# Packing two dQ blocks into one PSUM bank, with a new order of the backward attention loop

## The chip, the cores and the metric

The kernel runs on one core of one Trainium2 chip. The metric is the device time of one execution in microseconds (us); three runs of the kernel before gave 2509.24, 2516.67 and 2526.46 us, so the median is 2516.67 us. Durations and waits are read from one profiled execution, whose span is 2517.6 us.

## The reference

The reference is a transformer block with adaptive layer norm, and the gradient of its output with respect to ten inputs. Sizes: 2048 tokens, width 512, 32 heads of 16 columns, a hidden width of 1792. Cut to what matters here:

```
h = layernorm(x) * (1 + ca) + sa
q, k, v = split(h @ wqkv)                 # 32 heads x 2048 tokens x 16
p = softmax(q k^T * 0.25)                 # per head, 2048 x 2048
x = x + ga * ((p v) @ wo)
h = layernorm(x) * (1 + cb) + sb
x = x + gb * (relu(h @ w1 + b1)^2 @ w2 + b2)
out, grads = x, vjp(grad_out)             # grads of x, wqkv, wo, w1, b1, w2, b2, c, w_mod
```

The change lies in the attention's gradient. With E = exp(0.25 q k^T) as the forward pass scaled it, that gradient needs, for each head, dP = dO v^T, dS = E * dP (the row terms are folded into extra rows of the operands), dV = E^T dO, dK = dS^T q and dQ = dS k. Each of dP, E and dS is a 2048 x 2048 matrix per head and is recomputed tile by tile.

## The kernel before

Three stretches follow each other. The first 1120 us or so hold the projections, the forward attention and the dense part, forward and backward. From about 1126 us to 2390 us the **backward loop** runs, which the change rewrites. The last 127 us bring dQ, dK and dV through the projections to the outputs (`dh1`, `dwqkv`).

**How the loop is tiled.** Heads go in 8 groups (`hg`) of 4. For a group, keys go in 4 chunks (`kc`) of 512 and queries in 4 chunks (`qc`) of 512. One (hg, kc, qc) is a *block*; there are 128, numbered b, with qc running fastest. A block has four *units*, one for each 128 queries (`qi`). All 32-wide operands are packed four to the array: scores and dP use row tiles (32 rows of the array each), dK, dV and dQ use column tiles (32 columns each); four such products, one for each head of the group, are called a *quad*.

**What a unit does.** `score` (L1603) makes one head's 128x512 scores in a PSUM bank; `expo` (L1609) turns them into E on ACT. `dp_pair` (L1623) makes dP of two heads in one of two PSUM buffers `psD_u`, and DVE multiplies it with E into dS (L1625): this is called a *dS product* here, two to a unit, eight to a block. `k_quad` (L1663) and `v_quad` (L1672) add the unit to dK and dV in the bank `accVK`.

**How dQ is made.** dQ sums over keys, so dS has to be transposed. `transpose_unit` does that by DMA: SP issues one DMA transpose for two units (L1640) as soon as the second one's dS is there. In odd blocks the fourth unit is transposed on PE instead (`pe_turn`, L1653, 8 transposes at a time into a bank of the tag `px`, and an ACT copy, L1769), so that an odd block has one DMA transpose of two units and one of a single unit (L1638). A pair of blocks thus has three *doubles* and one *single* on SP's queue. The result is the tile `dsT`, three buffers of a block each. `dq_quad` (L1690) multiplies it with `KS_tok`, the keys by token, 32 columns from the head's first; the lower 16 are the head's, the upper 16 are those of the next head or zeros, and their result is not used. `dq_out` evicts the bank on ACT with the scale (L1700 for the first key chunk, L1703 later) and POOL adds it to `dQacc` (L1708). A finished group's dQ goes to DRAM by four DMAs issued by ACT (`load`, L1585), one after each of four consecutive dS products.

**What sets the order.** The loop is written out by hand in two strings of tokens, `order_n` and `order_t`, taken in turn: blocks b that follow an odd block use `order_t`, so even b use `order_t` and odd b `order_n`. Each engine takes its instructions in exactly this order. The tokens: `sI` a score, `eI` an exp, `D` the next dS product (with the DMA transpose that it completes, and with DMAs planned for its number by `at`), `q` the next `k_quad` or `v_quad`, `t1`/`T1`, `t2`/`T2` the two halves of `pe_turn` and their ACT copies for block b-1, `dI` two dQ quads, `Q` the eviction, `f` a product with zero weights into `accVK` (`keep_warm`, L1646). The dS products lag behind the scores by one `D` (`nD = -1`); in both orders `d1 d2 Q` work on block b-2. The letters of the second string say which of three score banks a score uses; bank C shares the tag `px` with `ptT` and `dqacc`.

DMAs of SP and ACT share eight semaphores, handed out in turn in program order. A DMA that gets a semaphore first waits until the DMA that had it before has landed, unless that is known to its queue already.

Of the kernel before, what the change touches and what calls it, by code (L numbers as in the profile page):

```python
# [20 lines left out]
P = 128  # L21
# [9 lines left out]
QPAD = 528  # L31
# [3 lines left out]
def kernel(  # L35
# [53 lines left out]
    k_st = dram.tile([P, TT, D], BF, name="k_st")  # L89
# [57 lines left out]
    with ExitStack() as ph:  # L147
# [848 lines left out]
        def plan_tasks():  # L996
# [72 lines left out]
            def token_tile(which, g, ti):  # L1069
# [9 lines left out]
                if which == 1:  # L1079
                    DVE.tensor_copy(T[key][:, ti, :], pt.rearrange("p b q -> p (b q)"))  # L1080
                    if ti == 3:
                        later(1, sp, k_st[:, gs, :], T[key][:])
                else:
                    tok = T[key].rearrange("p t d -> p (t d)").rearrange("p (g t e) -> p g t e", g=HG, t=4)
                    DVE.tensor_copy(tok[:, :, ti, :], pt.rearrange("p b q -> p (b q)").rearrange("p (g e) -> p g e", g=HG))
                    if ti == 3:
                        later(1, sp, q_st.rearrange("g p t e -> p g t e")[:, :, gs, :], tok)
# [125 lines left out]
        def kvq_loads(hg):  # L1213
            hs = hsets[hg % 2]
            for i in range(4):
                yield hs["qs"][:, 4 * i:4 * i + 4, :], q_st[hg][:, 4 * i:4 * i + 4, :]
# [4 lines left out]
        def spread_qz(hg):  # L1221
            to, fro = qz[hg % 2][:, :, :, DH:2 * DH], hsets[hg % 2]["qs"].rearrange("p t (h d) -> p t h d", h=4)
            if hg == 0:
                ACT.activation(to, fro, AF.Identity, scale=SCALE)
            else:
                POOL.tensor_scalar(to, fro, SCALE, None, ALU.mult)

# [14 lines left out]
        def last_chunk(O_c, L, w1T, w2T):  # L1242
# [127 lines left out]
            keep["KS"] = kpool.tile([P, TT, QPAD], BF, name="KS_tok", tag="ks")  # L1370
            POOL.memset(keep["KS"][:, :, D:QPAD], 0.0)
            for i in range(4):
                later(4 + 3 * i, sp, keep["KS"][:, 4 * i:4 * i + 4, 0:D], k_st[:, 4 * i:4 * i + 4, :])
# [171 lines left out]
    KS_tok, dOs_tok = keep["KS"], keep["dOs"]  # L1545
# [11 lines left out]
    with ExitStack() as ph:  # L1557
# [9 lines left out]
        def load_head(hg):  # L1567
            st = dict(hsets[hg % 2])
            st["qz"] = qz[hg % 2]
            st["acc"] = stg.tile([P, n], F32, name="dQacc", tag="dQacc", bufs=1)  # L1570
            st["dq"] = stg.tile([P, n], BF, name="dQst", tag="dQst", bufs=1)
            st["vk"] = stg.tile([P, n], BF, name="vkb", tag="vkb")
            hst[hg] = st


# [11 lines left out]
        def plan_head(hg):  # L1587
# [4 lines left out]
            at(j0 + 40, spread_qz, hg)  # L1592

# [12 lines left out]
        def expo(u, hq):  # L1606
            if hq == 0:
# [37 lines left out]
        def keep_warm():  # L1645
            PE.matmul(cur["vk"][0:DH, :], KS_tok[:, 0, D:QPAD], dOs_tok[:, 0, :], start=False, stop=False,  # L1646
# [35 lines left out]
        def dq_quad(b, kt):  # L1682
            hg, kc, qc, _ = units[4 * b]
            if kt == 0:
                cur["dq"] = psx.tile([P, 512], F32, name="dqacc", tag="px")
            acc = cur["dq"]
            tT = dqt[b]
            for hq in range(4):
                h = hg * 4 + hq
# [370 lines left out]
```

## Time and profile before

| | us |
|---|---|
| median of three runs | 2516.67 |
| span of the profiled execution | 2517.6 |
| first to last dS product of the loop | 1126.5 to 2382.3 |
| busy over the span: PE, ACT, DVE, POOL | 2342.5, 2302.3, 1810.1, 350.0 |
| busy in 1600 to 1800 us: PE, ACT, DVE | 192.49, 198.05, 191.12 of 200 |
| time of q1's (SP's) DMA packets, share of 16 engines' span | 82.2% |

The profiled execution's own time is its span; nothing measurable lies around it, as the median of the runs is within 1 us of it. An instruction's duration in the tables includes a part that overlaps with the next instruction on its engine, so rates are taken from the distance of starts in the timeline, not from durations.

### The profile page before, as it was taken

Reading aid. Unit: us, or ns where it says so; the run is one execution under the profiler, and the core shown is the slowest. Engines: PE = TensorE matmul, PEld = TensorE weight load, DVE = VectorE, ACT = ScalarE, POOL = GpSimd, SP = SyncE. Lnnn points to the kernel's source line nnn. Section 1 sums busy time; section 2 is a strip of 40 time slices with the busy share of each in tenths; the row PEclk is TensorE's granted clock in tenths of the full one; section 3 lists DMA queues with packets and bytes.
Section 4 is the critical chain, followed back from the end, with each engine's and each line's share of the span. In section 5 each row is a group of like instructions: output and inputs, shape, how many; then the busy total and the mean of one; then the engine's idle time right before and its main releaser. Section 6 shows DMA issues by size and latency. Waiting matters only on the chain. (4 is left out here: it accounts for less than half of the span.)

```text
span 2517.6 us, 49897 instructions
## 1 busy us (share of the span) xinstructions
PE 2342.5 (93%) x19005; PEld 776.3 (31%) x19005; DVE 1810.1 (72%) x2341; ACT 2302.3 (91%) x3577; POOL 350.0 (14%) x379
## 2 busy tenths in 40 slices
PE   7899889989988999999999999999999999999999
PEld 3232223222322323442233322233323323322343
DVE  5556153454435454579999999999999999998862
ACT  7999999999989999539999999999999999999842
POOL 2000000211323142210111101111010111100100
PEclk9999999999999999999999999999999999998999
DMA  6476455367658766979999999999999999999972
GB/s 202 136 193 165 150 122 139 96 161 144 103 85 176 151 134 119 261 208 191 202 199 210 196 206 208 201 207 202 207 202 202 209 195 203 195 208 212 196 237 72
DMA packets 1220981, 447.15 MB, mean 178 GB/s; under 512 B 1096951, under 2 KB 1191607, under 8 KB 1220486
## 3 DMA queue, kind: packets, MB, share of 16 engines
q1 hardware_dynamic: 1192822, 409.11, 82.2%
q0 software_dynamic: 10944, 16.78, 4.8%
q10 hardware_dynamic: 16976, 18.07, 2.8%
q8 instruction: 149, 2.44, 0.4%
q14 instruction: 90, 0.74, 0.1%
HBM read 96.75 MB, written 73.95 MB: 68 GB/s over the span
## 5 line engine op out<-in xcount | busy, mean ns | idle before, releaser
L1625 DVE TENSOR_TENSOR dS_u<-psD_u,E_u 128x1024 bf16<-128x1024 f32 x1024 | 1186.0, 1218 | 71.6 <-PE psD_u L1623 24.0
L567 ACT ACTIVATE ET<-psST 128x1024 bf16<-128x1024 f32 x1024 | 942.0, 1260 | 27.0 <-PE psST L565 26.5
L1609 ACT ACTIVATE E_u<-psS_A 128x512 bf16<-128x512 f32 x768 | 513.1, 668 | 10.5 <-PE psS_C L1603 8.5
L1609 ACT ACTIVATE E_u<-psS_B 128x512 bf16<-128x512 f32 x768 | 505.8, 659 | 12.1 <-DMA dsT<-dS_u 3.0
L1623 PE MATMUL psD_u<-iv,ido 32*128 32x512 bf16 x2048 | 409.6, 388 | 0.0
L565 PE MATMUL psST<-qt_sb,kt_sb 32*128 32x512 bf16 x2048 | 317.8, 387 | 62.0 <-ACT ET L567 46.6
L1609 ACT ACTIVATE E_u<-psS_C 128x512 bf16<-128x512 f32 x512 | 335.4, 655 | 3.3 <-PE psS_B L1603 1.4
L1603 PE MATMUL psS_B<-ik,iq 32*128 32x512 bf16 x768 | 295.3, 385 | 12.8 <-ACT E_u L1609 5.5
L1603 PE MATMUL psS_A<-ik,iq 32*128 32x512 bf16 x768 | 293.4, 382 | 10.9 <-DVE dwlast L237 1.0
L1603 PEld LDWEIGHTS <-iq 32*128 32x128 bf16 x2048 | 130.2, 91 | 316.1 <-issue 298.8
L1663 PE MATMUL accVK<-dS_u,qz 128*32 128x512 bf16 x2048 | 213.3, 390 | 0.4 <-PE psD_u L1623 0.2
L581 PE MATMUL oacc<-ET,vaug 128*32 128x512 bf16 x2048 | 207.7, 396 | 2.2 <-DVE ostage L585 2.2
L1672 PE MATMUL accVK<-E_u,dOs_tok 128*16 128x512 bf16 x2048 | 204.1, 387 | 0.0
L1708 POOL TENSOR_TENSOR dQacc<-dQacc,dqtmp 128x512 f32<-128x512 f32 x64 | 81.2, 1268 | 852.0 <-ACT dqtmp L1703 852.0
L1603 PE MATMUL psS_C<-ik,iq 32*128 32x512 bf16 x512 | 194.7, 380 | 4.2
L565 PEld LDWEIGHTS <-kt_sb 32*128 32x128 bf16 x2048 | 85.8, 91 | 352.2 <-issue 324.6
L1690 PE MATMUL dqacc<-dsT,KS_tok 128*32 128x512 bf16 x2048 | 146.5, 384 | 18.5 <-DMA dsT<-dS_u 4.3
L1769 ACT ACTIVATE dsT<-ptT 128x1024 bf16<-128x1024 bf16 x128 | 145.8, 1139 | 7.9 <-PE ptT L1653 7.3
L251 DVE COPY part<-pm 128x512 f32<-128x512 f32 (+2 forms) x103 | 63.5, 617 | 114.8 <-PE pm L233 111.5
L1623 PEld LDWEIGHTS <-ido 32*128 32x128 bf16 x2048 | 104.6, 91 | 98.9 <-issue 92.9
L1663 PEld LDWEIGHTS <-qz 128*32 128x32 bf16 x2048 | 58.4, 94 | 177.9 <-issue 162.9
L581 PEld LDWEIGHTS <-vaug 128*32 128x32 bf16 x2048 | 53.1, 93 | 121.4 <-issue 121.4
(407 smaller groups left out, 2516.3 us busy)
## 6 DMA issues: line engine op xcount, KB each, us to landing
p_st<-part POOLq DMA_DIRECT2D x36, 256.0 KB, 5.2
kt_sb<-qkT_st SPq DMA_DIRECT2D x124, 64.0 KB
wA<-in_B_w_dram SPq DMA_DIRECT2D x28, 256.0 KB
wB<-w1T_st SPq DMA_DIRECT2D x21, 256.0 KB
wA<-w2T_st SPq DMA_DIRECT2D x21, 256.0 KB
wB<-in_B_w_dram SPq DMA_DIRECT2D x21, 256.0 KB
p_st<-part POOLq DMA_DIRECT2D x25, 192.0 KB, 5.3
p_st<-part SPq DMA_DIRECT2D x18, 256.0 KB
```

Of the source, the lines that this page charges most:

```text
L565: PE.matmul(ps[:, hi, :], kt_sb[r:r + 32, kt * P:(kt + 1) * P], qt_sb[r:r + 32, :], start=True, stop=True, tile_position=(r, 0))
L567: ACT.activation(ET[:, 2 * pair:2 * pair + 2, :], ps[:], AF.Exp, scale=SCALE)
L581: PE.matmul(oacc[32 * hq:32 * hq + 32, :], lhsT, ET[:, hq, :], start=(kt == 0), stop=(kt == TT - 1), tile_position=(0, 32 * hq), skip_grou ...
L1603: PE.matmul(psS[:], st["q"][r:r + 32, qt * P:(qt + 1) * P], st["k"][r:r + 32, kc * 512:kc * 512 + 512], start=True, stop=True, tile_positi ...
L1609: ACT.activation(bst[u][0][:, hq, :], sst.pop((u, hq))[:], AF.Exp, scale=SCALE)
L1623: PE.matmul(psD[:, hi, :], st["do"][r:r + 32, qt * P:(qt + 1) * P], st["v"][r:r + 32, kc * 512:kc * 512 + 512], start=True, stop=True, til ...
L1625: DVE.tensor_tensor(dS_u[:, 2 * pair:2 * pair + 2, :], psD[:], E_u[:, 2 * pair:2 * pair + 2, :], ALU.mult)
L1663: PE.matmul(cur["vk"][32 * hq:32 * hq + 32, :], hst[hg]["qz"][:, qt, hq, :], bst[u][1][:, hq, :], start=(qt == 0), stop=False, tile_positi ...
L1672: PE.matmul(acc[32 * hq:32 * hq + DH, :], dOs_tok[:, qt, (hg * 4 + hq) * DH:(hg * 4 + hq + 1) * DH], E_u[:, hq, :], start=False, stop=(qt ...
L1690: PE.matmul(acc[32 * hq:32 * hq + 32, :], KS_tok[:, kc * 4 + kt, h * DH:h * DH + 32], tT[:, :, hq * 4 + kt, :], start=(kt == 0), stop=(kt ...
L1708: POOL.tensor_tensor(dst2, dst, tmp[:], ALU.add)
L1769: ACT.activation(dst, pt[:], AF.Identity)
```

## The change

1. Both blocks of a pair (two query chunks) put their dQ in one PSUM bank. The keys by token lie in two tiles `KZ` (one for even, one for odd groups), 16 columns of a head and 16 zero columns in turn, with 16 zeros ahead. The even block takes 32 columns from the head's own on, and fills the lower 16 rows of each quarter of the bank; the odd block takes them from the 16 before, and fills the upper 16. Eight quads accumulate, then one eviction and one POOL addition serve both. `dQacc` and `dQst` are half as wide.
2. `k_st` is stored by head group; each group's keys (256 KB) are loaded by ACT within the loop, as the first of the group's loads, and POOL spreads them (`spread_k`).
3. A finished group's dQ takes eight stores in place of four (`dq_rows`), each of 16 partitions; the last group's go through SP after the loop.
4. All `f` tokens go. `keep_warm` remains only in the first two blocks.
5. Both orders are new; `nD` starts at -2. `order_t` now holds `d1 d2 d3 d4 Q`, where `d1 d2` work on block b-2 and `d3 d4` on block b-1; `order_n` holds no dQ work. The loop has one trailing block in place of three.

```diff
+        def spread_k(hg):
+            to = keep["KZ"][hg % 2][:, :, DH:DH + 128].rearrange("p t (h e) -> p t h e", h=4)[:, :, :, 0:DH]
+            POOL.tensor_copy(to, keep["kst"].rearrange("p t (h d) -> p t h d", h=4))
...
+            at(j0 + 44, spread_k, hg)
...
         def dq_quad(b, kt):
             hg, kc, qc, _ = units[4 * b]
-            if kt == 0:
-                cur["dq"] = psx.tile([P, 512], F32, name="dqacc", tag="px")
-            acc = cur["dq"]
+            if "dq" not in cur:
+                cur["dq"] = [psx.tile([P, 512], F32, name="dqacc", tag="px"), 0]
+            acc, k = cur["dq"]
+            cur["dq"][1] += 1
             tT = dqt[b]
             for hq in range(4):
-                h = hg * 4 + hq
-                PE.matmul(acc[32 * hq:32 * hq + 32, :], KS_tok[:, kc * 4 + kt, h * DH:h * DH + 32], tT[:, :, hq * 4 + kt, :],
-                          start=(kt == 0), stop=(kt == 3), tile_position=(0, 32 * hq), skip_group_check=True)
+                lo = 32 * hq + DH * (1 - b % 2)
+                PE.matmul(acc[32 * hq:32 * hq + 32, :], KZ[hg % 2][:, kc * 4 + kt, lo:lo + 32], tT[:, :, hq * 4 + kt, :],
+                          start=(k == 0), stop=(k == 7), tile_position=(0, 32 * hq), skip_group_check=True)
...
-            if kc == QC - 1 and qc == QC - 1 and hg < HG - 1:
-                for hq in range(4):
-                    r = hg % 2 * 64 + hq * DH
-                    at(cur["j"] + 6 + hq, load, dQc[hg // 2, r:r + DH, :], st["dq"][32 * hq:32 * hq + DH, :])
+            if kc == QC - 1 and qc == QC - 2 and hg < HG - 1:
+                for i, (to, fro) in enumerate(dq_rows(dQc[hg // 2], hg, st["dq"])):
+                    at(cur["j"] + 6 + i, load, to, fro)
...
         order_t = (
-            "s0 s1 q s2 e0 e1 D s3 D e2 s4 e3 t1 e4 q T1 D "
-            "s5 s6 e5 f f t2 e6 s7 T2 e7 D s8 e8 D f f s9 e9 q q s10 "
-            "s11 e10 D d1 d2 e11 Q q s12 D e12 s13 e13 q s14 D e14 "
-            "s15 q q e15 ").split(), "ABCABBABACABABCA"
+            "s1 e1 D s2 e2 D s0 e0 s4 e4 q s3 e3 D t1 T1 s8 q e8 D s5 e5 D s7 e7 s6 e6 q s9 e9 "
+            "t2 T2 D D s11 s10 e10 e11 q d1 d2 s12 e12 D s13 e13 d3 d4 Q s14 e14 D s15 e15 ").split(), "CABBABACABBAABAB"
         order_n = (
-            "s0 D s1 q e0 q s2 e1 e2 D s3 s4 q s5 e3 D e4 "
-            "e5 s6 q s7 D s8 e6 e7 d1 e8 s9 D d2 e9 q Q s10 "
-            "s11 e10 D q s12 e11 e12 s13 e13 D q s14 s15 e14 e15 D q ").split(), "CBACBACBABABCABC"
+            "q q s0 e0 D s1 e1 q q s2 e2 D s3 e3 q q s4 e4 D s5 e5 q s7 e7 D s6 e6 q s14 e14 "
+            "s8 e8 D q s9 e9 s11 e11 D q s10 e10 s12 e12 q D s13 e13 s15 e15 q ").split(), "CABCABACCACBABBC"
...
-            nD, nq = -1, -4
+            nD, nq = -2, -4
...
-                        for kt in (2 * i - 2, 2 * i - 1):
-                            dq_quad(b - 2, kt)
+                        for kt in (2 * ((i - 1) % 2), 2 * ((i - 1) % 2) + 1):
+                            dq_quad(b - 2 + (i - 1) // 2, kt)
```

## The prediction

> **What bounds the kernel now.** I read the busy shares by stage first: in the backward loop PE, ACT and DVE are all over 95% busy, so only rates tell which of them could go faster. So next the timeline, for distances of starts.
>
> ```profile
> 1685.45 8.00 DVE L1625 TENSOR_TENSOR dS_u<-psD_u,E_u 128x1024 bf16<-128x1024 f32 x7
> ...
> 1708.46 0.60 ACT L1703 ACTIVATE dqtmp<-dqacc 128x512 f32<-128x512 f32 x1
> 1708.95 0.59 ACT L1609 ACTIVATE E_u<-psS_A 128x512 bf16<-128x512 f32 x1
> 1709.43 0.60 ACT L1609 ACTIVATE E_u<-psS_B 128x512 bf16<-128x512 f32 x1
> ...
> 1714.19 1.17 ACT L1769 ACTIVATE dsT<-ptT 128x1024 bf16<-128x1024 bf16 x1
> 1715.10 0.75 ACT L1609 ACTIVATE E_u<-psS_B 128x512 bf16<-128x512 f32 x1
> ```
>
> Seven dS products in 8.00 us, of which the last takes 1.22: (8.00 - 1.22) / 6 = 1.13 us each. An exp costs 0.48 (1709.43 - 1708.95), an eviction 0.49, a copy of transposed dS 0.91. A pair of blocks therefore needs at least 16 x 1.13 = 18.1 us of DVE, and 32 x 0.48 + 2 x 0.91 + 2 x 0.49 + 0.24 (half a `vkb`) = 18.3 us of ACT. From the start of every sixteenth dS product, an undisturbed pair takes 19.18 or 19.34 us in turn, 19.26 on average; all 63 intervals average 19.63. So DVE and ACT each have about 1 us of slack.
>
> SP's queue has less:
>
> ```profile
> 1698.21 2.88 SPq L1638 DMA_TRANSPOSE dsT<-dS_u  x1
> 1701.26 15.98 SPq L1640 DMA_TRANSPOSE dsT<-dS_u  x3
> 1717.33 3.06 SPq L1638 DMA_TRANSPOSE dsT<-dS_u  x1
> 1720.48 15.94 SPq L1640 DMA_TRANSPOSE dsT<-dS_u  x3
> 1736.51 1.73 SPq L1638 DMA_TRANSPOSE dsT<-dS_u  x1
> ```
>
> One row starts where the last ends: three doubles and a single, pair after pair.
>
> ```profile
> L1640 SPq DMA_TRANSPOSE dsT<-dS_u x192: 4769/5364/6827, 1133.2 to 2378.8; - x192
> ...
> L1638 SPq DMA_TRANSPOSE dsT<-dS_u x64: 1696/2592/4777, 1150.0 to 2383.8; - x64
> ```
>
> By the medians 3 x 5.36 + 2.59 = 18.7 us, and 4 x 0.1 between them: 19.05 of a pair's 19.26. Comparing each row's start with the end of the dS product it needs, 82% of the transposes start over 0.1 us late, up to 9.7 us. SP is as good as full, yet nothing waits for it: `dqacc` waits for `dsT` 4.3 us in the whole run. The reason is in the order: dQ of block b-2 comes at least 12 dS products (14.5 us) behind the last transpose that it needs.
>
> **The change, part by part.** *Packing.* 64 evictions and 48 POOL additions go: 64 x 0.49 = 31 us of ACT, 61 us of POOL. ACT's floor falls from 18.3 to 17.8 us a pair. SP's 19.05 and DVE's 18.1 stay, since the transposes and dS products are the same. So even perfect use of it gains (19.26 - 19.05) x 64 = 13 us.
>
> *Zero products.* About 256 of the 266 rows of L1646 go, at 0.22 to 0.32 us between starts: 1.1 us of PE a pair. PE is waiting elsewhere; I take 0, and price the clock under the rivals.
>
> *The order.* This is the term that decides. `d1 d2` on the even block are 12 products behind their transposes, as before. But `d3 d4` take the odd block b-1, whose single is issued after the last `D` of `order_n` (its unit 2); between that and `d3` stand eight `D`. PE reaches `d3` once it has issued the eighth; with two `psD` buffers this is when DVE has ended the sixth, 6 x 1.2 = 7.2 us, and some 0.5 us later. When does the single land? I read the time at which the semaphore of each transpose is full. From start to landing a double takes 8.25 us in the median (6.7 at least), a single 5.24 (4.29 at least); from the dS product that completes its data to its landing the single takes 10.4 (6.6 at least). So `d3` will wait, and PE takes its queue in order: behind `d3` are `d4 s14 D s15` and all of the next block; ACT then lacks scores, DVE its products.
>
> The wait closes a loop, which gives the new period. Let `d3` start at X. Four quads at 0.215 and a change of tiling (0.33) bring the next `D` at X + 1.0; DVE starts 0.5 later. The product after it needs E of `e15`: `Q` starts on ACT 0.43 after the last quad (X + 1.07), `e14` and `e15` follow at 0.49 and 0.48, and `e15`'s 0.6 and that product's 1.22 end it near X + 3.95. These two are the last products of the even block, and let SP start that block's second double. From the start of this double over the odd block's double to the landing of its single, the 63 cases of the trace take 16.1 us on average (median 15.9, 5% at 14.9, 95% at 17.8, least 14.3). Then the next `d3` can start: X + 3.95 + 15.9 = 19.85. I take 0.1 less, 19.75, since the single may land a little sooner with less queued behind it: singles followed by over 0.5 us of an idle queue landed 2.43 us after their issue ended, those with less 2.8 to 2.9. Against 19.26 this is +0.49 x 64 = **+31 us**. The bounds: with the fast chain 3.95 + 14.9 = 18.85, under SP's 19.05 (-13); with the slow mean 20.05 and variations that are not made up for, about 20.3 (+67).
>
> *The stores of dQ.* Eight semaphores serve all DMAs, so eight stores and the loads among them, one `D` apart, soon ask for one that a transpose still holds. In the changed kernel's order, the fifth DMA of each group's batch waits for a double completed 7 dS products before, and a load three products later for one 6 products before. Before, the shortest was 9 products, once a group, and it cost this:
>
> ```profile
> 1464.14 0.59 ACT L1609 ACTIVATE E_u<-psS_A 128x512 bf16<-128x512 f32 x1
> 1467.36 0.34 ACTq L1585 DMA_DIRECT2D dQc<-dQst  x1
> 1467.76 0.60 ACT L1609 ACTIVATE E_u<-psS_B 128x512 bf16<-128x512 f32 x1 [3.03 <-DMA dsT<-dS_u]
> ```
>
> A store stands in front of an exp until a transpose lands. A double takes 8.25 us from its start and starts at once or late; 7 products are 8.4 us, of which ACT runs ahead one or two. So each of the two waits is about 2 us. Behind them stand the exps; PE's scores fill their three banks and stop. Part is made up before `d3`: I take 2 us a group, 7 groups, less the one of before: 14 - 3.9 = **+10** (0 to 30).
>
> *Moves at nothing.* 35 more ACT DMA issues of 0.3 to 0.4 us lie beside running activations (at 1700.78 one stands between starts 0.49 apart); uncovered they are 12 us. `spread_k` is like the spread of `qz`, 2.77 us on a POOL that is 14% busy, and is due some 80 products before its use. The longer `KZ` fill (4608 columns against 1.80 us for 2048, 4.1 us) stands ahead of four fills that nothing waits for early. `k_st` is written as `q_st` is, and a pass of either takes 0.42. Three key loads less ahead of the loop: nothing waited for them.
>
> *The end.* SP issues eight stores of the last dQ in place of four; its four take 3.04 us (L1793), and the chain of waits runs through SP's next loads: **+2** (0 to 4).
>
> Sum: 2517.6 + 31 + 10 + 2 = 2560.6, **2560 us**, 1.7% over the median.
>
> **The rivals.** *A, the forecast*: `d3` waits for the single in nearly every pair. For it speaks that the transposes keep their lengths whatever waits around them: doubles that found an idle queue took 5.4 us as well. 2535 to 2605, chance 0.57.
>
> *B, the transposes land in time*: the fast chain becomes the rule, SP's rate sets the pair at 19.05, -13 + 10 + 2 gives 2517, or 2500 to 2530. It decides if chains stay under 15.1 us, as 7 of the trace's 63 do. Chance 0.20.
>
> *C, on the other side: the transposes themselves get shorter*, as the queue's back-pressure ends. Doubles then take 4.9, their lower mode, and the single 1.8: 3 x 4.9 + 1.8 + 0.4 = 16.9 us, and DVE's 18.1 with 0.45 of waits is the bound, 18.55: -45 + 2 and no waits of stores, 2475 to 2490. It decides when the chain is under about 14.5 us. Against it: doubles after idle. Chance 0.12. The Trainium skill (DMA: Bandwidth & Descriptors, Latency and other measured facts) states 261 GB/s for DMA transposes; a double's 1.05 MB would be an estimated 4.0 us by that, and this case would follow. The trace does not agree: 5.36 us.
>
> *D, the clock.* In the loop the granted clock falls to half seven times, six of them for 3.41 us:
>
> ```profile
> 1845.40:1848.70 3.30, 3.20 (x25) 0.88 (x22) 3.03 (x4) 3.30 (x8) 0.20 (x1) 1.00 1.25 289
> 1848.80:1852.10 3.30, 3.30 (x18) 0.98 (x17) 2.85 (x3) 2.95 (x5) 0.00 (x0) 0.50 1.25 218
> ```
>
> The column after the busy times is the clock. The five falls without a long stall each follow 3.4 us that hold two quads and at most three transposes, the other products being 32-row ones; stretches with two quads and eight transposes kept the clock. Such a pair takes 1.3 us more (20.51 for 19.18). The new order has three `D` between the last quad of a block pair's second block and `t1`, with one quad among them, and no `f`; so falls may come in half of the pairs, 32 x 1.3 = 40 us. In A they lie mostly beside SP's chain, so I add nothing there. Where they don't: 2600 to 2625, chance 0.11. The Trainium skill (TensorE: Matmul & The Clock Gate, Part 1: The HAM clock gate) says that activity over a window of about 3.4 us releases the clock and an idle one halves it; the trace agrees with the window, 3.41 us, but shows falls with PE busy 3.20 of 3.30 us.
>
> That the change does not do what it says can be left aside: in the order of the changed kernel 257 matmuls and 64 evictions are gone. (Half of each dQ product's columns are still zero, at no more time than before.)
>
> **How the numbers follow.** A, at 2560, is the likeliest. The range **2497 to 2605** leaves out C and most of D. No change means within 1% (2492 to 2542), about what a measurement of this kernel can tell: B and the low end of A, 0.25. Faster is C, 0.12. Slower is the rest, 0.63.
>
> **What would show it.** Right: `dqacc` idle until a DMA of `dsT`, 0.5 to 2 us in most pairs, where it was 4.3 us in all; pairs near 19.8 us; ACT idle before exps, released by `dsT`, twice a group; SP's rows with a gap of about 1 us in each pair. L1646 nearly empty and half as many rows of `dqtmp`. Wrong: pairs at or under 19.2 us, doubles near 4.9 us, or a granted clock under 0.95 over the loop.

## The result

The changed kernel takes **2607.63 us** (median; 2592.34 to 2614.46) against 2515.37 us of the kernel before on the same chip: a ratio of **1.0357, 95% interval 1.0312 to 1.0401**. It is slower, as forecast, by more than twice the 1.7% of the forecast. Its profiled execution has a span of 2612.5 us, 94.9 more than before. Of these, 90.8 lie in the backward loop: from its first to its last dS product it takes 1345.4 us, where it took 1254.6. What follows takes 136.3 us, where it took 136.4. The rest lies ahead of the loop, which begins at 1130.8 us for 1126.5; in the runs below it begins anywhere from 1123 to 1133 us.

First the groups of instructions of the dS and dQ products, before and then after (columns: busy us, mean ns of one, idle us just before, and what ended it):

```profile
L1625 DVE TENSOR_TENSOR dS_u<-psD_u,E_u 128x1024 bf16<-128x1024 f32 x1024 | 1186.0, 1218 | 71.6 <-PE psD_u L1623 24.0 <-PE psS_A L1603 11.5 <-PE psS_B L1603 10.5
L1690 PE MATMUL dqacc<-dsT,KS_tok 128*32 128x512 bf16 x2048 | 146.5, 384 | 18.5 <-DMA dsT<-dS_u 4.3 <-ACT E_u L1609 1.1
```

```profile
L1637 DVE TENSOR_TENSOR dS_u<-psD_u,E_u 128x1024 bf16<-128x1024 f32 x1024 | 1185.3, 1215 | 164.3 <-PE psS_B L1615 61.1 <-ACT E_u L1621 39.6 <-ACT dqtmp L1718 30.5
L1703 PE MATMUL dqacc<-dsT,KZ_tok 128*32 128x512 bf16 x2048 | 155.9, 431 | 70.5 <-DMA dsT<-dS_u 61.5 <-ACT dsT L1780 8.4 <-DMA iv<-vT_st 0.3
```

PE's dQ products, which waited 4.3 us for transposes, wait 61.5 us. DVE's products are as long as before (1215 ns for 1218) and wait 164.3 us, for 71.6. Now SP's queue of transposes in the timeline after the change, and its doubles by source line (least, median and longest in ns):

```profile
1686.07 16.57 SPq L1652 DMA_TRANSPOSE dsT<-dS_u  x3
1702.74 2.27 SPq L1650 DMA_TRANSPOSE dsT<-dS_u  x1
1705.17 19.05 SPq L1652 DMA_TRANSPOSE dsT<-dS_u  x3
1724.32 3.13 SPq L1650 DMA_TRANSPOSE dsT<-dS_u  x1
1729.63 17.13 SPq L1652 DMA_TRANSPOSE dsT<-dS_u  x3
```

```profile
L1652 SPq DMA_TRANSPOSE dsT<-dS_u x192: 4806/5126/7159, 1136.3 to 2474.0; - x192
```

The rows are no longer end to end: the fourth ends at 1727.45 and the fifth starts at 1729.63. Such pauses between transposes sum to 15 to 24 us in a group of eight pairs, where they were 3 to 11. A double is no longer than it was (median 5.13 us for 5.36). So the queue that was full did not become slower; it is given its work later. One pair shows why (timeline, all engines; the rows of other tiles left out):

```profile
1702.74 2.27 SPq L1650 DMA_TRANSPOSE dsT<-dS_u  x1
...
1704.75 1.05 PE L1703 MATMUL dqacc<-dsT,KZ_tok 128*32 128x512 bf16 x16 [0.18 <-ACT dsT L1780]
...
1708.98 1.90 PE L1703 MATMUL dqacc<-dsT,KZ_tok 128*32 128x512 bf16 x16 [2.85 <-DMA dsT<-dS_u]
...
1710.93 0.60 ACT L1718 ACTIVATE dqtmp<-dqacc 128x512 f32<-128x512 f32 x1 [3.69 <-PE dqacc L1703]
...
1711.56 1.23 DVE L1637 TENSOR_TENSOR dS_u<-psD_u,E_u 128x1024 bf16<-128x1024 f32 x1 [4.07 <-ACT dqtmp L1718]
```

The sixteen products of `d1 d2` take 1.05 us. `d3 d4` stand still for 2.85 us until the odd block's single, started at 1702.74, has landed; ACT then has waited 3.69 us and DVE 4.07. And sixteen products of the same kind now take 1.90 us: at 1708.79, at the end of the wait, PE's granted clock fell to half for 3.41 us.

That is the second thing that the profile after shows. Over the middle of the loop, before and after (columns: PE, its weight loads PEld, DVE, ACT and POOL busy, each with its count; then the granted clock, the share of the DMA engines and GB/s):

```profile
1200.00:2300.00 1100.00, 1057.50 (x10155) 331.14 (x10152) 1045.03 (x904) 1081.12 (x2061) 124.28 (x91) 0.99 1.18 204
```

```profile
1200.00:2300.00 1100.00, 980.72 (x9164) 298.77 (x9160) 963.71 (x834) 972.53 (x1849) 75.03 (x54) 0.92 1.09 189
```

834 dS products against 904 in the same 1100 us, at a clock of 0.92 against 0.99. In the whole loop the clock fell 27 times and stood at half for 201 us; before it was 8 times (the seven of the forecast and one at the loop's first product) and 44 us.

Third, the stores of dQ. ACT's timeline after the end of a group:

```profile
1658.38 0.60 ACT L1621 ACTIVATE E_u<-psS_A 128x512 bf16<-128x512 f32 x1
1661.74 0.33 ACTq L1596 DMA_DIRECT2D iqs<-q_st  x1
1662.11 0.59 ACTq L1596 DMA_DIRECT2D dQc<-dQst  x1
1662.74 0.60 ACT L1621 ACTIVATE E_u<-psS_B 128x512 bf16<-128x512 f32 x1 [3.77 <-issue]
```

A load and a store stand between two exps, and ACT does nothing for 3.77 us. The trace gives the reason: the load has the semaphore of a transpose that SP started at 1651.42 and that landed at 1661.72, and only then is the load issued. Such idle times beside DMA issues sum to 33 us in the loop (6 before).

### The profile page after: what moved, and what is told of

Same layout as the page of the kernel before. It is cut to its first block, busy times and chain, and to the rows that moved or that the text cites. A ratio compares the mean times of both kernels' runs of the same rounds, so it can differ in the third digit from the quotient of the medians.

```text
span 2612.5 us, 49244 instructions
## 1 busy us (share of the span) xinstructions
PE 2345.1 (90%) x18748; PEld 767.7 (29%) x18748; DVE 1810.4 (69%) x2341; ACT 2269.6 (87%) x3513; POOL 301.6 (12%) x339
## 3 DMA queue, kind: packets, MB, share of 16 engines
q10 hardware_dynamic: 19776, 19.91, 2.7%
## 4 chain that ended last, share of the span: by engine, by line
PE 53%; DMA 14%; ACT 14%; DVE 11%; issue 5%; SPq 1%; POOL 0%; ACTq 0%; DVEq 0%; POOLq 0%
DMA dsT<-dS_u 12%; ACT ET L567 9%; DVE dS_u L1637 6%; PE accVK L1675 5%; PE psS_A L1615 4%; PE psST L565 4%; PE psD_u L1635 4%; PE dqacc L1703 4%; ACT E_u L1621 4%; PE psS_C L1615 3%; PE accVK L1684 3%; PE psS_B L1615 3%; PE pm L233 3%; PE oacc L581 2%; PE pdh L1895 2%
## 5 line engine op out<-in xcount | busy, mean ns | idle before, releaser
L1637 DVE TENSOR_TENSOR dS_u<-psD_u,E_u 128x1024 bf16<-128x1024 f32 x1024 | 1185.3, 1215 | 164.3 <-PE psS_B L1615 61.1
L1621 ACT ACTIVATE E_u<-psS_A 128x512 bf16<-128x512 f32 x768 | 490.8, 639 | 39.5 <-PE psS_B L1615 29.7
L1635 PE MATMUL psD_u<-iv,ido 32*128 32x512 bf16 x2048 | 421.2, 401 | 39.0 <-DVE dS_u L1637 35.0
L1615 PE MATMUL psS_B<-ik,iq 32*128 32x512 bf16 x768 | 307.4, 400 | 23.0 <-ACT E_u L1621 22.7
L1615 PE MATMUL psS_A<-ik,iq 32*128 32x512 bf16 x768 | 306.5, 399 | 5.9 <-ACT E_u L1621 1.6
L1703 PE MATMUL dqacc<-dsT,KZ_tok 128*32 128x512 bf16 x2048 | 155.9, 431 | 70.5 <-DMA dsT<-dS_u 61.5
L1615 PEld LDWEIGHTS <-iq 32*128 32x128 bf16 x2048 | 119.3, 92 | 273.3 <-issue 266.1
L1635 PEld LDWEIGHTS <-ido 32*128 32x128 bf16 x2048 | 120.4, 91 | 203.5 <-issue 181.0
L1780 ACT ACTIVATE dsT<-ptT 128x1024 bf16<-128x1024 bf16 x128 | 136.1, 1063 | 8.7 <-PE ptT L1665 7.0
L1723 POOL TENSOR_TENSOR dQacc<-dQacc,dqtmp 128x512 f32<-128x512 f32 x32 | 40.7, 1270 | 716.0 <-ACT dqtmp L1718 716.0
L1703 PEld LDWEIGHTS <-KZ_tok 128*32 128x32 bf16 x2048 | 55.7, 103 | 141.5 <-DMA dsT<-dS_u 62.2
```

The source lines that it names most:

```text
L1615: PE.matmul(psS[:], st["q"][r:r + 32, qt * P:(qt + 1) * P], st["k"][r:r + 32, kc * 512:kc * 512 + 512], start=True, stop=True, tile_positi ...
L1621: ACT.activation(bst[u][0][:, hq, :], sst.pop((u, hq))[:], AF.Exp, scale=SCALE)
L1635: PE.matmul(psD[:, hi, :], st["do"][r:r + 32, qt * P:(qt + 1) * P], st["v"][r:r + 32, kc * 512:kc * 512 + 512], start=True, stop=True, til ...
L1637: DVE.tensor_tensor(dS_u[:, 2 * pair:2 * pair + 2, :], psD[:], E_u[:, 2 * pair:2 * pair + 2, :], ALU.mult)
L1703: PE.matmul(acc[32 * hq:32 * hq + 32, :], KZ[hg % 2][:, kc * 4 + kt, lo:lo + 32], tT[:, :, hq * 4 + kt, :], start=(k == 0), stop=(k == 7), ...
L1780: ACT.activation(dst, pt[:], AF.Identity)
```

## The experiments

Sixteen kernels were run. For each: the median time, the ratio to before with its 95% interval, and from its profile the mean pair of blocks, the median pair with no fall of the clock starting in it or in the one before it ("quiet"), the falls in the loop with the time at half clock, and PE's wait of dQ products for DMA transposes. Each ratio is to the kernel before in the same batch of runs, where its median was 2515 to 2523 us; times of different batches are compared to some 8 us.

| kernel | us | ratio | mean pair | quiet pair | falls, us at half | wait for `dsT` |
|---|---|---|---|---|---|---|
| before | 2515.37 | 1 | 19.63 | 19.31 | 8, 44 | 4.3 |
| changed | 2607.63 | 1.0357 (1.0312 to 1.0401) | 21.07 | 19.25 | 27, 201 | 61.5 |
| no_wait | 2549.81 | 1.0121 (1.0074 to 1.0168) | 20.08 | 18.69 | 12, 164 | 0.3 |
| zeros_back | 2593.21 | 1.0301 (1.0249 to 1.0353) | 20.78 | 19.57 | 18, 137 | 42.1 |
| stores_apart | 2577.99 | 1.0256 (1.0191 to 1.0320) | 20.55 | 19.48 | 21, 140 | 74.8 |
| before_no_zeros | 2555.93 | 1.0148 (1.0099 to 1.0196) | 20.21 | 19.24 | 48, 177 | 2.2 |
| no_wait_apart | 2523.25 | 1.0023 (1.0008 to 1.0038) | 19.63 | 18.69 | 14, 150 | 3.2 |
| no_wait_zeros_apart | 2523.60 | 1.0013 (0.9997 to 1.0029) | 19.63 | 19.12 | 8, 79 | 0.0 |
| packing_alone | 2571.77 | 1.0215 (1.0197 to 1.0234) | 20.48 | 19.91 | 20, 82 | 2.1 |
| late_dq_apart | 3127.22 | 1.2424 (1.2401 to 1.2447) | 29.16 | none | 119, 1126 | 0.0 |
| late_dq_apart_zeros | 3210.02 | 1.2749 (1.2716 to 1.2781) | 30.37 | none | 113, 1004 | 1.1 |
| two_later_apart | 2670.14 | 1.0595 (1.0570 to 1.0621) | 22.06 | 19.80 | 36, 358 | 4.1 |
| two_later_apart_zeros | 2652.31 | 1.0542 (1.0516 to 1.0569) | 21.63 | 20.25 | 14, 174 | 5.2 |
| two_later_spread | 2674.74 | 1.0622 (1.0596 to 1.0649) | 22.15 | 19.82 | 41, 369 | 2.7 |
| two_later_spread_pool | 2609.26 | 1.0367 (1.0334 to 1.0400) | 21.05 | 19.82 | 12, 174 | 26.7 |
| after_pool_dma | 2639.54 | 1.0483 (1.0460 to 1.0506) | 21.50 | 19.28 | 29, 232 | 115.5 |
| before_pool_dma | 2535.95 | 1.0069 (1.0040 to 1.0097) | 19.89 | 19.34 | 7, 48 | 11.2 |
| before_stores_apart | 2530.20 | 1.0049 (1.0027 to 1.0071) | 19.69 | 19.34 | 6, 41 | 4.7 |

### One cause at a time

**The wait.** The odd block's quads read the even block's transposes, which landed long before. All products are still issued; the odd block's dQ is left out of the result.

```diff
-            tT = dqt[b]
+            tT = dqt[b - b % 2]
```

> The changed kernel, but the dQ quads of the odd block read the even block's transposed dS, which has landed long before; the odd block's dQ is left out that way. Every instruction and its place in the queues stay, only the wait of d3 for the last transpose goes. If that wait is the main cause: its 61.5 us on PE and most of the falls of the clock that follow it go, 2525 to 2550 us, a mean pair of 19.4 to 20.0 us. If the falls of the clock come from the order alone: 20 to 27 falls stay and the time is over 2570 us. If the stores of dQ were the main cause: little changes, over 2580 us.

Measured: 2549.81 us, 57.8 less than the changed kernel. A quiet pair now takes 18.69 us. So the wait is the largest single cause. The falls of the clock go from 27 to 12, but the time at half clock only from 201 to 164 us, so most of that time does not come from this wait. And the run is still slower than before by 1.2%, though its quiet pairs are 0.6 us shorter: the two pairs in which a group's stores are issued take 23.5 and 24.0 us on average.

**The zero products.** Two `f` each are put back ahead of `s3` and ahead of the third `q` of `order_t`.

```diff
-"s1 e1 D s2 e2 D s0 e0 s4 e4 q s3 e3 D t1 T1 s8 q e8 D s5 e5 D s7 e7 s6 e6 q s9 e9 "
+"s1 e1 D s2 e2 D s0 e0 s4 e4 q f f s3 e3 D t1 T1 s8 q e8 D s5 e5 D s7 e7 s6 e6 f f q s9 e9 "
```

> The changed kernel with four products of zero weights in each order_t, as before, two ahead of s3 and two ahead of the third q, to keep PE active. If the clock is the main cause: hardly any falls are left, 2530 to 2560 us. If the wait of d3 is the main cause: the wait on the transposes stays at 55 to 75 us and the time falls by 10 to 35 us only, 2570 to 2600 us. If the stores are: 2590 us or more.

Measured: 14 us less, nine falls and 64 us at half clock fewer, and a wait for transposes of 42.1 us, under the 55 to 75 expected. The intervals of the two ratios overlap, so this alone does not show that zero products pay in the new order. The next run does, in the old one.

**The zero products of before**, taken away and nothing else:

```diff
-"s5 s6 e5 f f t2 e6 s7 T2 e7 D s8 e8 D f f s9 e9 q q s10 "
+"s5 s6 e5 t2 e6 s7 T2 e7 D s8 e8 D s9 e9 q q s10 "
```

> The kernel before without the four products of zero weights in each order_t; nothing else changes. If these products are what keeps the clock up: falls of the clock in 15 or more pairs in place of 7 in all, and 2530 to 2560 us. If the clock falls only because PE waits for transposes: within 6 us of the kernel before, up or down, with fewer than 10 falls.

Measured: 1.0148 times before, and 48 falls for 8. Four stretches of 3.30 us in order of time (the clock is the column after the busy times):

```profile
1487.30:1490.60 3.30, 3.22 (x28) 1.15 (x27) 3.19 (x3) 3.30 (x8) 0.00 (x0) 1.00 1.23 145
1490.70:1494.00 3.30, 2.34 (x25) 1.06 (x23) 3.20 (x4) 3.30 (x6) 0.00 (x0) 1.00 1.11 256
1494.10:1497.40 3.30, 3.30 (x29) 0.84 (x32) 2.71 (x3) 2.89 (x6) 0.00 (x0) 0.50 0.87 162
1497.50:1500.80 3.30, 3.21 (x41) 0.72 (x34) 2.40 (x3) 3.02 (x6) 0.00 (x0) 1.00 1.15 215
```

The stretch in which PE was busy 2.34 us is followed by one at half clock, in which DVE falls from 3.20 busy to 2.71. A pair in which a fall starts takes 20.43 us in the median, a quiet one 19.24: 1.2 us a fall, and it comes in 47 of 63 pairs. The zero products of before were no idle work.

**The stores**, four dS products apart in place of one:

```diff
-                    at(cur["j"] + 6 + i, load, to, fro)
+                    at(cur["j"] + 6 + 4 * i, load, to, fro)
```

> The changed kernel with the eight stores of a group's dQ four dS products apart in place of one, so that none asks for a semaphore that a fresh transpose holds. If the stores cost what the trace of the changed kernel shows (about 24 us of ACT idle beside them): 2575 to 2590 us. By the price of the prediction (2 us a group): 2590 to 2597 us. If all of it is made up before d3: no change, 2600 to 2610 us.

Measured: 2577.99 us, 30 us less by the medians and 25 by the ratios, whose intervals just overlap. ACT's idle time beside DMA issues goes from 33 us to 0. The waits of the dQ products became longer (74.8 for 61.5), so part of what the stores no longer take goes to waits for transposes.

### The causes together

No wait and stores apart (again the odd block's dQ is left out, with all products issued); then the zero products too.

> The changed kernel without the wait of d3 (the odd block's dQ is left out as in no_wait) and with the stores of dQ four dS products apart. In no_wait the pairs away from the stores take 18.69 us and the two at a group's end 24 to 25 each, some 10 us a group too much. If wait and stores are the two large causes and the falls of the clock in no_wait come mostly from the stores: 64 x 18.7 and some falls, 2475 to 2500 us, faster than the kernel before. If the falls come from the order itself: 15 or more remain and the time is 2500 to 2530 us.

> The run that has no dQ of the odd block (its quads read the even block's transposes, so the outputs that need dQ are not the reference's) and its stores apart, with the four zero products a pair back. Its undisturbed pairs took 18.69 us, and 14 falls of the clock, 150 us at half clock, brought the mean to 19.63. Theory 1, the falls come from missing zero products: at most 6 falls, mean pair under 19.1, 2480 to 2500. Theory 2, they come with the stalls at the ends of groups: 10 or more falls, 2515 to 2530.

Measured: 2523.25 and 2523.60 us, 1.0023 and 1.0013 times before. So the wait and the stores together account for 84 of the 92 us, each with the falls of the clock that go with it. What is left is of more interest. The first run has quiet pairs of 18.69 us, 0.6 under before, yet its mean pair is that of before, 19.63, and 14 falls hold the clock at half for 150 us. The falls need not be the whole reason: in the quiet pairs SP's queue takes 19.25 us (median) from a pair's first transpose to the next pair's, so it falls behind, and such pairs cannot follow each other for long. The second run has 8 falls, but its quiet pairs take 19.12; that a zero product costs PE something once no wait covers it would fit. The first expectation had the falls nearly right in its second alternative (15 or more falls, 2500 to 2530 us). Both theories of the second expectation missed: fewer falls, as the one said, and no time, as the other did. So with the wait gone, and with the odd block's dQ left out, the packed loop in this order reaches the time of the old one and no more.

### The packing alone

The order and the zero products of before; only `d1 d2` and `d3 d4` stand in one `order_n`, on blocks b-3 and b-2, both transposed long before. The key loads in the loop and the eight stores stay as in the changed kernel, the stores four apart.

```diff
-"e5 s6 q s7 D s8 e6 e7 d1 e8 s9 D d2 e9 q Q s10 "
+"e5 s6 q s7 D s8 e6 e7 d1 d2 e8 s9 D d3 d4 e9 q Q s10 "
```

> The packing of two blocks' dQ with the order of the kernel before and its zero products: only d1 d2 Q are taken out of order_t, and order_n has d1 d2 and d3 d4 in place of d1 and d2, on blocks b-3 and b-2; stores four products apart. If packing is harmless and its gain small, as the rate of SP's queue would have it (13 us at most): 2500 to 2520 us, few falls of the clock. If packing is at fault: over 2540 us.

Measured: 1.0215. Not a wait for transposes (2.1 us), and most of it not the clock: the quiet pair is 0.6 us longer (19.91). The groups show where:

```profile
L1637 DVE TENSOR_TENSOR dS_u<-psD_u,E_u 128x1024 bf16<-128x1024 f32 x1024 | 1193.9, 1218 | 117.1 <-PE psD_u L1635 51.5 <-PE psS_A L1615 19.1 <-ACT dqtmp L1718 14.7
L1718 ACT ACTIVATE dqtmp<-dqacc 128x512 f32<-128x512 f32 x48 | 28.7, 597 | 24.6 <-PE dqacc L1703 24.6
```

DVE waits 51.5 us for PE's `psD_u` (24.0 before), ACT 24.6 us for the dQ bank. Eight quads around one dS product, where four stood in each of two blocks, seem to keep PE from scores and dP for longer than the two buffers of `psD` last; no run tells this place apart from the packing itself. The stores and loads have a part as well: the second and third pair of a group take 21.7 and 22.4 us on average.

### dQ later

Can the order be mended? The first try moves all of dQ to the middle of `order_n` and takes four `q` from there into `order_t` to make room (stores apart; the second run has four zero products as well).

```diff
-"t2 T2 D D s11 s10 e10 e11 q d1 d2 s12 e12 D s13 e13 d3 d4 Q s14 e14 D s15 e15 "
+"t2 T2 D D s11 s10 e10 e11 q q q s12 e12 D s13 e13 q q s14 e14 D s15 e15 "
...
-"... q q s4 e4 D s5 e5 q s7 e7 D s6 e6 q s14 e14 "
+"... s4 e4 D s5 e5 q s7 e7 D s6 e6 d1 d2 d3 d4 Q s14 e14 "
```

> The changed kernel with its dQ work (d1 to d4 and Q) moved from order_t to the middle of the next order_n, where it works on blocks b-3 and b-2, four q moved the other way, and the stores four products apart; nothing is left out. d3 then stands 13 dS products behind its last transpose in place of 8. If the tight wait was the fault of the change and not the packing: no waits on the transposes, pairs of 18.7 to 19.2 us, 2480 to 2520 us. If the packing itself costs time (a bank held for eight quads): 2530 us or more.

> late_dq_apart with four products of zero weights in each order_t, two ahead of s3 and two ahead of the third q. If the missing zero products cost time in this order as well: 10 to 30 us less than late_dq_apart, with fewer falls of the clock; if the four q moved into order_t keep the clock up on their own: within 8 us of it.

Measured: 1.2424 and 1.2749, far outside every expectation. The first run's groups:

```profile
L1675 PE MATMUL accVK<-dS_u,qz 128*32 128x512 bf16 x2048 | 348.3, 509 | 187.2 <-DVE dS_u L1637 149.4 <-ACT vkb L1687 36.6
```

The moved `q` come too early. Counted in the orders, in the changed kernel at least one more dS product is issued between the product that a `k_quad` needs and the `k_quad`; here it is none at two places of each pair. PE waits 149.4 us for DVE, which waits for PE in turn, and the clock stands at half for 1126 us of the loop. No pair of these runs has the full clock, so what the order would cost at full clock can't be read from them, and the runs say nothing on the theories that they were meant to tell apart.

The second try leaves every `q` in its place and moves only `d3 d4 Q`, by two dS products (one `D` ends `order_t`, one stands ahead of them in `order_n`):

```diff
-"... s12 e12 D s13 e13 d3 d4 Q s14 e14 D s15 e15 "
+"... s12 e12 D s13 e13 s14 e14 D s15 e15 "
...
-"q q s0 e0 D s1 e1 q q s2 e2 D s3 ..."
+"q q s0 e0 D d3 d4 Q s1 e1 q q s2 e2 D s3 ..."
```

> The changed kernel with the stores of dQ four dS products apart, and with d3 d4 Q moved behind the first D of order_n (the odd block's quads two dS products later; the scores in front of them use banks A, B). Theory 1, the wait for the odd block's transpose is what the packing costs, and it is only short: 61.5 us of waits over 64 pairs is 0.96 us a pair, and two dS products are 2.4 us, so PE's wait for dsT falls under 15 us in all, and the time is near that of the run without the odd block's dQ, 2515 to 2535. Theory 2, the transposes' queue sets the pair and the wait moves along with the place of d3 (the later start lets the queue fall back as well): the wait stays over 30 us, and the time is that of the run with the stores apart alone, 2560 to 2590.

> As the run with d3 d4 two dS products later, and four zero products a pair back in order_t (ahead of s3 and of the third q). Theory 1, what is then left above the undisturbed pair are falls of the clock that follow stretches with few products on the whole array: the falls go from about 14 to 8 or fewer and the time is 10 to 30 us under that run, 2490 to 2515. Theory 2, the falls follow the stalls at the ends of the groups, which zero products do not shorten: as many falls, the same time within 6 us.

Measured: the wait goes, as theory 1 said (4.1 us), and the time **rises** to 2670.14 and 2652.31 us. Both theories fell. Two things took the wait's place. A quiet pair takes 19.80 us, 1.1 more than without a wait at the old place; one of the sixteen intervals between its dS products is 2.15 us long, where most are 1.13:

```profile
1594.23 0.39 PE L1635 MATMUL psD_u<-iv,ido 32*128 32x512 bf16 x2
1594.55 1.05 PE L1703 MATMUL dqacc<-dsT,KZ_tok 128*32 128x512 bf16 x16
...
1595.85 0.40 PE L1675 MATMUL accVK<-dS_u,qz 128*32 128x512 bf16 x4
1596.07 0.39 PE L1684 MATMUL accVK<-E_u,dOs_tok 128*16 128x512 bf16 x4
...
1596.39 0.39 PE L1635 MATMUL psD_u<-iv,ido 32*128 32x512 bf16 x2
```

Six quads stand between the two dP pairs: four of dQ, one of dK and one of dV. And the pairs early in a group are far longer. Means by a pair's place in its group of eight (groups 2 to 8):

| | 1 | 2 | 3 | 4 | 5 | 6 | 7 | 8 |
|---|---|---|---|---|---|---|---|---|
| before | 19.7 | 20.2 | 19.3 | 19.2 | 20.0 | 19.5 | 19.5 | 19.4 |
| changed | 21.5 | 24.2 | 19.2 | 23.2 | 20.3 | 19.8 | 20.9 | 19.6 |
| stores_apart | 19.8 | 22.2 | 20.4 | 22.1 | 20.0 | 19.5 | 21.6 | 19.5 |
| no_wait_apart | 18.8 | 19.7 | 20.7 | 20.9 | 18.9 | 19.7 | 18.7 | 18.7 |
| two_later_apart | 21.1 | 26.5 | 27.1 | 22.5 | 20.4 | 19.8 | 20.3 | 19.8 |
| two_later_spread_pool | 21.1 | 23.7 | 20.8 | 20.6 | 19.8 | 21.2 | 21.4 | 19.8 |
| after_pool_dma | 18.8 | 28.3 | 19.3 | 23.0 | 20.3 | 21.7 | 20.2 | 19.8 |

Pairs 1 to 4 are those in which the old group's dQ is stored and the next group's operands are loaded. Before has hardly a trace of it; the packed kernels of the table have. In the third pair of a group of this run (ACT):

```profile
1705.84 0.60 ACT L1621 ACTIVATE E_u<-psS_A 128x512 bf16<-128x512 f32 x1 [1.11 <-PE psS_B L1615]
1705.85 0.32 ACTq L1596 DMA_DIRECT2D ik<-qkT_st  x1
1706.21 1.17 ACTq L1596 DMA_DIRECT2D dQc<-dQst  x1
1707.42 0.60 ACT L1621 ACTIVATE E_u<-psS_B 128x512 bf16<-128x512 f32 x1 [0.98 <-PE psD_u L1635]
```

The store's issue takes 1.17 us between two exps here, and for 0.98 us of it ACT's engine is idle. Such idle times sum to 35 us in this run although its stores are four products apart; in the run stores_apart, with `d3` in its old place, they were 0.3 us. The next run keeps the place and has four quads between any two dP pairs:

```diff
-"q q s0 e0 D d3 d4 Q s1 e1 q q s2 e2 D s3 e3 q q s4 e4 D ..."
+"q q s0 e0 D d3 d4 Q s1 e1 s2 e2 D q q s3 e3 q q s4 e4 D ..."
```

> As the run with d3 d4 two dS products later, but the two quads that followed them go behind the next D, so that four quads and no longer six stand between two dS products. Theory 1, the six quads made the 0.9 us by which its undisturbed pairs (19.80) lay above those without a wait (18.7 to 18.8): the undisturbed pairs come down to 18.8 to 19.2, and the time by 0.7 x 64 = 45 us or more, to 2570 to 2625. Theory 2, the place costs what it costs because ACT's eviction now stands between the exps of the next block's first unit: pairs stay at 19.6 to 19.9, 2655 to 2675.

Measured: 2674.74 us, and quiet pairs of 19.82, whose long interval is still 2.06 us. Theory 1 fell: the count of quads is not what makes this place dear. The idle time of DVE that ended with `psS_C` (87 us, now 7) now ends with `E_u` (119 us, for 53). That ACT's eviction between the exps of the next block's first unit is the cause agrees with it, but no run took the eviction away, so it stays open.

### Who issues the loads and stores

The loop's loads and stores are issued by POOL, which is 12% busy, in the changed kernel, in the last order, and in before:

```diff
         def load(to, fro):
-            ACT.dma_start(out=to, in_=fro)
+            POOL.dma_start(out=to, in_=fro)
```

> The changed kernel with one edit: the loop's loads and stores are issued by POOL in place of ACT, at the same places. Theory 1, ACT's waits for semaphores that transposes hold make the long pairs of the first half of a group (first four pairs of a group: 21.5, 24.2, 19.2, 23.2 us): these fall to 19.5 to 21.5, ACT's idle time beside DMA issues goes from 33 us to 0, and the time is that of the run with the stores apart or less, 2545 to 2580; the waits of d3 stay near 60 us. Theory 2, the traffic of these DMAs holds up the transposes, whoever issues them: the same pairs stay long, 2595 to 2615.

> Both edits, d3 d4 two dS products later with four quads between dS products, and the loop's loads and stores issued by POOL; the stores are not spread. Theory 1, all that the packed loop loses are the wait for the odd block, the quads in one place and ACT's waits beside DMA issues: pairs of 18.8 to 19.2 throughout the group, 20 falls of the clock or fewer, 2480 to 2520, which would be before or better. Theory 2, the loop is also held up by the traffic, or by falls of the clock that no wait explains: the first pairs of a group stay over 21 us, 2540 to 2600.

> The kernel before with the loop's loads and stores issued by POOL. Theory 1, ACT is freed of 29 issues of 0.3 to 0.4 us and of a 3 us stall a group, but its queue and the transposes were not what set the pair: within 10 us of before. Theory 2, ACT's issues cost it what they last (12 us in the loop) and the stall 3 us a group: 15 to 30 us less, 2488 to 2503.

Measured in the changed kernel: ACT's idle time beside DMA issues falls to 0, and the kernel becomes **slower** by 32 us (2639.54), beyond the 2615 of the second theory. PE's wait for transposes nearly doubles, to 115.5 us. POOL's timeline at the end of a group, then SP's, then PE's dQ products:

```profile
1658.88 1.05 POOL L1596 DMA_DIRECT2D dQc<-dQst  x2
1659.89 0.63 POOL L1596 DMA_DIRECT2D KZ_tok<-k_st  x1
1660.47 2.04 POOL L1596 DMA_DIRECT2D dQc<-dQst  x4
1662.43 0.65 POOL L1596 DMA_DIRECT2D iqs<-q_st  x1
```

```profile
1654.11 22.48 SPq L1652 DMA_TRANSPOSE dsT<-dS_u  x3
1676.63 6.20 SPq L1650 DMA_TRANSPOSE dsT<-dS_u  x1
```

```profile
1684.93 1.90 PE L1703 MATMUL dqacc<-dsT,KZ_tok 128*32 128x512 bf16 x16 [8.28 <-DMA dsT<-dS_u]
```

With nothing to hold it, POOL issues six stores and two loads within 4.2 us. The three doubles then take 22.48 us and the single 6.20, where the rows of the changed kernel above have 16.57 and 2.27, and `d3` waits 8.28 us. In the first pair of groups 2 to 8 a double lands 11.9 us after its start (mean), where it was 8.5 with ACT as the issuer. So this burst holds up the transposes. That ACT's waits for semaphores had kept the transfers apart fits this, but it was not tried by itself. Nor is it shown that the same burst from ACT would do the same: the profile lists POOL's transfers in a queue of another kind (software, q0) than ACT's and SP's (hardware). The Trainium skill (Trainium Kernel Development and Optimization, Key Constraints) says that DMAs of all queues run on the same 16 engines, so that issuing them from another engine saves issue time alone; the run agrees so far, as ACT's idle time went to 0 and transposes of SP's queue got longer beside POOL's transfers.

In the order with `d3` two products later, which can bear a late transpose, the same edit, with the stores one product apart again, gains 65 us (2674.74 to 2609.26). ACT's 34 us of idle time beside DMA issues go, and the falls go from 41 to 12. It is still 3.7% over before, and over both theories. Before itself loses 0.7% by it, more than the 10 us of its first theory. The last run sets the stores of before four products apart:

```diff
-                    at(cur["j"] + 6 + hq, load, ...)
+                    at(cur["j"] + 6 + 4 * hq, load, ...)
```

> The kernel before with one edit, its four stores of a group's dQ four dS products apart. Theory 1, an ACT wait for a store's semaphore of 3 to 4 us costs the loop what it lasts, as the 30 us of the changed kernel's stores suggest: 7 groups by 3 us, 15 to 25 us less, 2492 to 2502. Theory 2, such a stall is made up by the slack of ACT and DVE in the pairs behind it: within 6 us of before.

Measured: 1.0049, slower if anything. But there was little to win. Both expectations took a stall of 3 us of ACT in each group of before; its trace has one such stall in the whole loop (3.03 us at 1467.8), and six of 0.3 to 0.7 us, 6 us in all. With the stores apart they are 8 us. So this run does not show what removing such a stall gives. No kernel tried beats before.

## Why the prediction was right or wrong

The direction was right; the time, 2607.63, lies 48 us above the forecast and just outside its range. Two terms of the sum were too small, the clock and the stores. From one `d3` to the next the 63 pairs of the changed kernel take 80 us more than 63 times the 19.75 forecast, where the forecast had left 33: 23 for the uneven pairs of before and 10 for the stores. Of the 80, 44 lie in the seven pairs across a group's end, and 25 in the 48 pairs in which `d3` waits as forecast.

**What bounds the kernel: right as to the neck.** Quiet pairs of 18.69 us, where nothing waits, seem to refute "SP's 19.05 stay". They do not: in the same pairs of no_wait SP's queue takes 19.21 us a pair (median), and from the second to the seventh pair of a group its lag behind the dS products grows from 0.03 to 2.2 us. The queue has no fixed rate, though: in the run no_wait_apart, where it is late nearly throughout, its pair takes 19.6 to 20.8 us in the first six places of a group, and 18.1 and 18.6 in the last two.

**The wait of `d3`: mechanism right, and its price nearly.** In 48 of 63 pairs of the changed kernel `d3` starts within 0.15 us of the landing of the odd block's single. Such a pair takes 20.27 us, where 19.75 was forecast. The chain from the even block's second double to that landing was taken as 15.8 to 15.9 us and is 16.0; the way from `d3` to the start of that double was taken as 3.95 us and is 4.04 at full clock, but 4.69 in the 13 pairs in which the clock is at half for a part of it. PE's idle time is 61.5 us, 0.96 a pair, but not "0.5 to 2 us in most pairs": 19 of 64 lie in that range, 12 above it. Taking the wait away gives 58 us where +31 was forecast. The two do not measure quite the same, since without the wait the new order has shorter pairs than before.

**The clock at nothing: the first step that failed.** "In A they lie mostly beside SP's chain, so I add nothing there." Of the signs of being wrong that the prediction named, this one came true: the clock over the loop is 0.92, under 0.95. Rival D had the price of a fall right (1.3 us a pair forecast, 1.2 measured in before without zero products), and nearly the number (half of the pairs; 24 of 63). But it was set up as an alternative to A, and the two hold together. Ten of the 23 waits of more than 1 us have a fall between 1 us before their end and 3.5 us after it, as in the pair shown above, and half speed makes PE later at the next dP. By the forecast's own numbers A and D together are 2560 + 40 = 2600 us. What the falls alone cost the changed kernel was not measured clear of noise: zeros_back took 64 us at half clock away for 14 us, with overlapping intervals. The Trainium skill (TensorE: Matmul & The Clock Gate, Part 1: The HAM clock gate) describes a free-running window of 3413 ns; the falls of these runs agree with it: in the run with dQ two products later two of them start at 1500.82 and 1511.06, three such windows apart. How long PE is busy in such a window does not decide alone. Cut on this grid, the changed kernel keeps its clock after 14 windows in which PE was busy for less than 2.6 us (1.72 the least), and loses it after five in which it was busy for 3.09 to 3.12.

**The stores at 2 us a group: the second step that failed.** The single waits are of the forecast size or longer (2 forecast, up to 3.77), and the reason of the four over 3 us, a semaphore that a transpose holds, is the forecast one. But the pair across a group's end, from its last `d3` to the next group's first, takes 24.8 to 27.5 us. The seven of them hold 44 us more than seven pairs of 19.75, where the forecast gave 14. "Part is made up before `d3`" failed: the stall brings a fall of the clock each time, and these seven falls hold the clock at half for 82 of the loop's 201 us. Setting the stores apart gives back 25 to 30 us of it, since the wait for transposes grows.

**The rest.** The end costs 0, not 2. No run shows a gain from the evictions and POOL additions that go; the forecast gave them none. The terms taken out one by one (58, 25 to 30, 14) sum to 97 to 102 us of a difference of 92, so they overlap a little, and nothing large seems to be missing. That the first four pairs of a group, not the steady pair, hold most of the loss (the table of places) was not foreseen: but for its 10 us for the stores, the forecast priced one pair and multiplied by 64.

## What to carry to other kernels

Before packing two results into one buffer, ask which of the two is ready last: the shared step takes the later one's time, and a lead of 14.5 us that covered everything became one of 7.2 us, and `d3` waited in most pairs. Rivals that can be true together have to be priced together, here a wait of PE and the falls of its clock. And where a queue runs full, look at the stretches in which other transfers join it (here the first four of eight pairs of a group), not only at the steady state.

## What the runs showed of the hardware that was not expected

- In each of six traces (before, before_no_zeros, changed, zeros_back, no_wait_apart, late_dq_apart) all falls of the clock in the loop start on one grid of 3.413 us and last whole steps of it. PE's busy share of a step does not settle whether one comes: in before the clock fell after five steps in which PE was busy for 3.29 us or more, in the changed kernel it stayed after one with 1.72.
- Four zero products a pair, some 1 us of PE, kept 40 falls away and were worth 1.5% of the kernel (interval 1.0 to 2.0).
- With six stores and two loads put out within 4.2 us by POOL, three transposes of two units took 22.48 us in place of 16.57, and in the first pairs of groups they landed 11.9 us after their start (mean) in place of 8.5.
- A loop in which PE waits for DVE directly can stay at half clock: 1126 of 1864 us in the run with the moved `q`, with a time 24% above before.
